# Polynomial-sketch attention and an ELU feed-forward on one core: the head of the program reordered

## The chip, the core and the metric

The kernel runs on one core of a Trainium2 chip. A core has five engines that run their own instruction streams and wait for each other by semaphores: PE (TensorE, matrix products; its weight loads are shown as PEld), DVE (VectorE), ACT (ScalarE), POOL (GpSimd) and SP (SyncE, which here only issues DMAs). ACT issues a few DMAs too. The metric is the device time of one execution in microseconds (us).

## The reference

q, k, v and the output are float32. The sketch matrices S1 and S2 and the two weights arrive as float64, and the kernel rounds them to float32 itself (see below).

```python
# q, k, v: (4, 4, 1088, 32)   S1, S2: (8, 32)   w_in: (128, 2048)   w_out: (2048, 128)
def phi(x):
    a = einsum('rd,bhsd->bhsr', S1, x)
    b = einsum('rd,bhsd->bhsr', S2, x)
    return einsum('bhsi,bhsj->bhsij', a, b).reshape(..., 64)
kv  = einsum('bhsf,bhsd->bhfd', phi(k), v)
z   = sum(phi(k), axis=2)
x   = einsum('bhsf,bhfd->bhsd', phi(q), kv) / (einsum('bhsf,bhf->bhs', phi(q), z) + 1e-6)
x   = x.transpose(0, 2, 1, 3).reshape(4352, 128)
h   = x @ w_in
g   = where(h > 0, h, exp(min(h, 0)) - 1)
out = g @ w_out
```

For each of four batches b, the keys and values of the whole sequence must be summed into kv and z before any query of that batch can be finished; the feed-forward part then takes the rows of x in groups.

## The kernel before

**Tiling.** The 4 x 1088 rows of x are 68 half tiles of 64 rows; eight of them make a group g of 512 rows (nine groups, the last has 256). The 2048 hidden columns are eight pairs cp of two blocks of 128. A step is one (g, cp): `mm1` makes two 128x512 blocks of h on PE, `elu` makes e on ACT (a relu of -h, then an exp) and gg on DVE, and `mm2` adds the pair's contribution into o on PE. The main loop runs `mm1` of step n, then the extra work hung on that step, `elu` of step n, and `mm2` of step n-2.

**The order is written out by hand.** Nothing is rescheduled: each engine runs its instructions in the order in which the source issues them, and the semaphores come from the tiles' dependences. So where a call stands in the source decides what it is queued behind on its engine.

**The head** is what stands before that loop (L603 to L647). It makes the first kv and z, the first group of x and the first two steps:

- The loads are issued first: S1 and S2, the keys of batch 0 in two parts (SP takes half tiles 0 to 8, ACT the others), eight half tiles of queries (`load_hd`, L143 and L144, SP one half and ACT the other, 128 KB each), v of batch 0 in two parts (`load_v(0)`), and then the weights pair by pair between the rest of the queries and the next batches. A DMA semaphore is one of eight in turn; a load waits until the load eight places before it in the list has landed.
- `keep_warm(n, cols)` multiplies a constant tile into a PSUM tile called idle that nobody reads (L223): n products of cols columns that only keep PE working.
- DVE rounds S (L102 to L128) and copies it to Sx. PE turns it (sps, L252, and SXps, L244), and DVE makes Sab of it (L254).
- `transp` on DVE (L237) turns the loaded keys and queries into kT and qT.
- `KF` (L276): products abp of kT and Sab; `KF_out` copies them to ab on ACT (L285); `KO` (L261) makes the outer products kp on DVE, in three parts; `KA` (L309) sums kp and v into kv on PE; `KC` (L321), `KZ1` (L330), `KS` (L345) and `KZ2` (L337) prepare kv and z for the queries.
- The first group of queries goes another way than the later ones: `q1_first` (abqp, L417, and abq, L421), `q2_first` (qp, L261), `q4_first` (transposes qtp, L434, and their copies qpT, L435), `q5_first` (x0ps, L456; dn and xn on DVE; x0tp, L471; xg, L472), `mm1_first` (L536).
- `x0_eps` (L441) opens the sums in x0ps: two products of one row (128x264 out, one partition in) put the 1e-6 of the reference into the two PSUM tiles to which L456 adds.

**Rounding of the weights.** The weights arrive as 64-bit words in raw; each is turned into float32 in five steps: `round_a` (DVE, L102), `round_b` (ACT, L107), `round_c` (DVE, L115 and L116), `round_d` (DVE, L120) and `round_e` (DVE, L128, or POOL for later pairs). RA(i), RB(i) and RC(i) are steps a, b and c to e of the i-th piece in the list `order` at L167. Pieces 0 and 1 are w_in of pairs 0 and 1, pieces 2 and 3 are w_out of pairs 0 and 1, piece 4 is w_in of pair 2.

**The second half of the head** (L625 to L647) interleaves the rounding of pieces 1, 2 and 3 with e and gg of steps (0,0) and (0,1), and with the second group of queries: `q2(1, 2)` (DVE, qp in two halves), `q4(1)` (transposes L486, copies L487), `q5(1, True)` (xps, L507) and `q5_out` (xg, ACT L518 and DVE L519), then one more `keep_warm(1)`. The main loop's first product is `mm1(1, 0)`; RC(3) hangs on its first step, RA(4) and RB(4) follow on that step, and RC(4) hangs on the next; piece 4 is first needed at `mm1(0, 2)`.

Of the kernel before, what the change touches and what calls it, by code (L numbers as in the profile page):

```python
# [27 lines left out]
def kernel(  # L28
# [19 lines left out]
    nc = tc.nc  # L48
# [18 lines left out]
    hd = {}  # L67
# [3 lines left out]
    kT = [const.tile([FD, NT, 64], F32, name=f"kT{b}") for b in range(B)]  # L71
    qT = [const.tile([FD, NT, 64], F32, name=f"qT{b}") for b in range(B)]

    def load_hd(eng, x, src, b, t0, t1, c=slice(0, 2)):
        if (x, b) not in hd:
            hd[x, b] = work.tile([P, 2, NT, D], F32, name="hd_" + x, tag="hd_" + x)
        eng.dma_start(hd[x, b][:, c, t0:t1, :],
                      src[b].rearrange("h (a c t) d -> (h a) c t d", a=32, c=2)[:, c, t0:t1, :])

    def load_v(b, engs=(nc.sync, nc.sync)):  # L80
        for u, eng in enumerate(engs):
            t0, t1 = u * KT, min(NT, u * KT + KT)
            r = slice(64 * u, 64 * u + 64)
            src = v[b].rearrange("h (y t) d -> y h t d", t=NT)[:, :, t0:t1, :]
            if b == 0:
                eng.dma_start(vt[b][r, :VN].rearrange("p (h t d) -> p h t d", h=H, t=KT)[:, :, :t1 - t0, :], src)
            else:
                for h in range(H):
                    eng.dma_start(vt[b][r, h * KT:h * KT + t1 - t0, :D], src[:, h])
# [50 lines left out]
            eng.dma_start(S16[rs, :], src)  # L140
    load_hd(nc.sync, "k", k, 0, 0, KT)
    load_hd(nc.scalar, "k", k, 0, KT, NT)
    load_hd(nc.sync, "q", q, 0, 0, 8, slice(0, 1))  # L143
    load_hd(nc.scalar, "q", q, 0, 0, 8, slice(1, 2))  # L144
    load_v(0)
    warm = const.tile([R, 1], F32, name="warm")
    nc.vector.memset(warm[:], 0.0)
# [21 lines left out]
    def round_w(f, i, *a):  # L169
        if wide:  # L170
            cp, w_in, w_out = order[i]
            c = slice(0 if w_in else 2 * P, 4 * P if w_out else 2 * P)
            f(raw_w[cp][:, c], W[:, cp, c], *a)

    def RA(i):
        round_w(round_a, i)

    def RB(i):
        round_w(round_b, i)

    def RC(i, pool=False):
        round_w(round_c, i)
        round_w(round_d, i)
        round_w(round_e, i, pool)
# [36 lines left out]
    def keep_warm(n, cols=256):  # L221
        for i in range(n):
            nc.tensor.matmul(idle[:, :cols], some[:, :P], some[:, :cols], skip_group_check=True)  # L223
# [12 lines left out]
    def transp(dst, x, b, t0, t1):  # L236
        nc.vector.transpose(dst[b][:, t0:t1, :].rearrange("p t (a c) -> p c t a", c=2), hd[x, b][:, :, t0:t1, :])  # L237
# [10 lines left out]
    Sab = const.tile([FD, H, 2 * R], F32, name="Sab")  # L248
    SW = const.tile([FD, B, H, 3, R], F32, name="SW")
    keep_warm(3)  # L250
    sps = psum.tile([P, 512], F32, name="sps", tag="aux")
    nc.tensor.matmul(sps[:, :2 * R], Sx[:].rearrange("p h d -> p (h d)"), ident[:2 * R, :2 * R])  # L252
    make_SX()
# [34 lines left out]
    def KO(b, gi):  # L288
        ab, rows = feats[b, gi]
        n = len(KG[gi])  # L290
        kp = work.tile([P, 4, H, R, R], F32, name="kp", tag="kp", bufs=3)
        outer(kp[:rows, :n].rearrange("p t h i j -> p (t h) i j"),
              ab[:rows, :n].rearrange("p t h x r -> p (t h) x r"))
        feats[b, gi] = kp, rows
# [62 lines left out]
    def half_tile(g, i, u):  # L357
        return divmod(8 * g + (2 * i + u if g < NQ - 1 else u * qn[g] + i), NT)
# [33 lines left out]
    def q2(g, parts=1):  # L392
        m = H * qn[g]
        x = abw[g][:, :m, :]
        pw = pws[g % 2]
        nc.vector.tensor_mul(pw[:, :m, :R], x[:, :, R:2 * R], x[:, :, 2 * R:])
        den = work.tile([P, 4 * H], F32, name="den", tag="den")
        nc.vector.tensor_reduce(den[:, :m], pw[:, :m], axis=AX, op=ADD)
        nc.vector.reciprocal(den[:, :m], den[:, :m])
        an = work.tile([P, 4 * H, R], F32, name="an", tag="an")  # L400
        nc.vector.tensor_mul(an[:, :m], x[:, :, R:2 * R], _ap(den[:, :m], [[1, m], [0, R]]))
        qp[g] = work.tile([P, 4 * H, R, R], F32, name="qp", tag="qp", bufs=2)
        for i in range(parts):
            h = slice(i * m // parts, (i + 1) * m // parts)
            a_ = an[:, h]
            b_ = x[:, h, :R]
            nc.vector.tensor_mul(qp[g][:, h], _ap(a_, list(a_.ap[1:]) + [[0, R]]),  # L407
                                 _ap(b_, [b_.ap[1], [0, R], b_.ap[2]]))
# [3 lines left out]
    def q1_first():  # L412
        p = psum.tile([P, 512], F32, name="abqp", tag="aux")
        for i in range(4):
            for u in range(2):
                b, t = half_tile(0, i, u)
                nc.tensor.matmul(p[64 * u:64 * u + 64, i * 64:i * 64 + 64], qT[b][:, t, :],  # L417
                                 Sab[:].rearrange("p h y -> p (h y)"),
                                 skip_group_check=True, tile_position=(0, 64 * u))
        x = work.tile([P, 4 * H, 2, R], F32, name="abq", tag="abq", bufs=1)  # L420
        nc.scalar.copy(x[:].rearrange("p m x r -> p (m x r)"), p[:, :4 * 64])  # L421
        abw[0] = x
# [14 lines left out]
    def x0_eps():  # L437
        xps = []
        for tt in range(2):
            p = psum.tile([P, 512], F32, name="x0ps", tag="h", bufs=4)  # L440
            nc.tensor.matmul(p[:, :8 * (D + 1)], some[:1, :P], eps[:].rearrange("p m d -> p (m d)"),  # L441
                             start=True, stop=False, skip_group_check=True)
            xps.append(p)
        return xps
# [45 lines left out]
    def q5(g, between=False):  # L490
        nh = qn[g] // 2
        xp = [psum.tile([P, 512], F32, name="xps", tag="aux") for _ in range(2)]

        parts = {0: [], 1: []}
        for w in range(2):
            for m in range(nh):
                b, b1 = (half_tile(g, 2 * m + w, u)[0] for u in range(2))
                if b != b1:
                    parts[w] += [(b, m, 1, slice(0, 64)), (b1, m, 1, slice(64, P))]
                elif parts[w] and parts[w][-1][0] == b and parts[w][-1][3] == slice(0, P):  # L500
                    parts[w][-1] = (b, parts[w][-1][1], parts[w][-1][2] + 1, slice(0, P))
                else:
                    parts[w] += [(b, m, 1, slice(0, P))]
        for h in range(H):
            for w in range(2):
                for b, m0, m, s in parts[w]:
                    nc.tensor.matmul(xp[w][D * h:D * h + D, :nh * P].rearrange("p (m s) -> p m s", s=P)[:, m0:m0 + m, s],  # L507
                                     kvS[64 * w:64 * w + 64, b, h, :], qpT[g][64 * w:64 * w + 64, h, m0:m0 + m, s],
                                     skip_group_check=True, tile_position=(64 * w, D * h))
        xg[g] = work.tile([P, 512], F32, name="xg", tag="xg", bufs=2)  # L510
        if not between:
            q5_out(g, xp)
        return xp

    def q5_out(g, xp):
        nh = qn[g] // 2
        to = xg[g][:, :2 * nh * P].rearrange("p (m w s) -> p w m s", w=2, s=P)
        nc.scalar.copy(to[:, 0], xp[0][:, :nh * P].rearrange("p (m s) -> p m s", s=P))  # L518
        nc.vector.tensor_copy(to[:, 1], xp[1][:, :nh * P].rearrange("p (m s) -> p m s", s=P))  # L519
# [11 lines left out]
    def mm1_first():  # L531
        hs[0, 0] = [psum.tile([P, 512], F32, name="h", tag="h", bufs=4) for c in range(2)]
        for tt in range(2):
            for c in range(2):
                s = slice(256 * tt, 256 * tt + 256)
                nc.tensor.matmul(hs[0, 0][c][:, s], W[:, 0, c * P:c * P + P], xg[0][:, s], skip_group_check=True)  # L536

    def elu_a(g, cp, c, parts=(0, 1)):

        n = qn[g] * P  # L540
        if c == 0 and 0 in parts:
            es[g, cp] = work.tile([P, 2, 512], F32, name="e", tag="e", bufs=2)
        e = es[g, cp][:, c, :n]
        if 0 in parts:
            nc.scalar.activation(e, hs[g, cp][c][:, :n], RELU, scale=-1.0)  # L545
        if 1 in parts:
            nc.scalar.activation(e, e, EXP, scale=-1.0)  # L547
# [52 lines left out]
            eng.dma_start(rows[b, :, t:t + n, :], o[64 * u:64 * u + 64])  # L600


    keep_warm(2, 192)  # L603
    transp(kT, "k", 0, 0, KT)
    transp(kT, "k", 0, KT, NT)
    KF(0)
# [1 line left out]
    transp(qT, "q", 0, 0, 8)  # L608
    KO(0, 0)
    q1_first()  # L610
    x0 = x0_eps()
    KO(0, 1)
    KO(0, 2)
    RA(0)
# [8 lines left out]
    q5_first(x0)  # L623
    mm1_first()
    RC(1)  # L625
    for c in range(2):
        elu_a(0, 0, c)
    mm1(0, 1)
    q2(1, 2)
    RA(2)  # L630
    RB(2)
    q4(1)
    for c in range(2):
        elu_d(0, 0, c)
    round_w(round_c, 2)
    x1 = q5(1, True)
    elu_a(0, 1, 0, (0,))
    q5_out(1, x1)
    keep_warm(1)
    elu_a(0, 1, 0, (1,))  # L640
    elu_a(0, 1, 1)
    round_w(round_d, 2)
    round_w(round_e, 2)
    for c in range(2):
        elu_d(0, 1, c)
    RA(3)
    RB(3)  # L647

# [106 lines left out]
```

## Time and profile before

| | us |
|---|---|
| median of 5 runs (290.19 to 291.64) | 291.29 |
| the profiled execution | 291.05 |
| its span, first to last instruction | 289.3 |
| PE busy in the span | 282.9 |
| ACT, DVE busy | 187.2, 166.4 |
| first key product abp (L276) starts | 6.88 |
| first product of the main loop (L529) starts | 24.05 |

Times in the profile count from the start of the span. A row of a timeline is a run of like instructions of one engine: start, time from the first start to the last end, engine, source line, operation, what it writes and reads, shape, count, and in brackets how long the engine had been idle and what released it. A float32 product is two records on PE. Records of PE overlap: what counts is the distance between starts, not a record's length, in which the way through the array is contained.

### The profile page before, as it was taken

To read this page: it belongs to the slowest core of one execution; us is meant where nothing else is said; L and a number is where in the kernel's file an instruction comes from. 1 tells how busy PE (TensorE), PEld (TensorE's weight loads), DVE (VectorE), ACT (ScalarE), POOL (GpSimd) and SP (SyncE) were. 2 spreads that over 40 slices of the span, in tenths; PEclk is the share of its full clock that TensorE was granted. 3 is DMA by queue.
4 is the path that set the end of the run, shared out by engine and by line. 5 is a ranking of instruction groups with operands and counts; after the bars stand their busy time and mean duration, and the time that the engine had idled before them with its cause. 6 is when DMAs were issued, how large, how long until landed. Compare 5 with 4: busy or idle time off the path is not lost.

```text
span 289.3 us, 3955 instructions
## 1 busy us (share of the span) xinstructions
PE 282.9 (98%) x1432; PEld 148.9 (51%) x1432; DVE 166.4 (58%) x298; ACT 187.2 (65%) x357; POOL 17.1 (6%) x49
## 2 busy tenths in 40 slices
PE   8999999999999999999999999999999999999994
PEld 5874354545544755445444554444445544444694
DVE  6887999794865393545355443464442654355442
ACT  2468878476575565656676658665766676568682
POOL 3100003433000101000000000000000000000000
PEclk9999999999999999999999999999999999999999
DMA  6997894200004000002001100020002000100020
GB/s 181 346 260 188 192 222 48 77 0 0 2 0 62 13 0 3 0 6 35 0 0 20 17 2 0 1 35 2 0 0 36 2 2 0 25 11 0 6 33 18
DMA packets 37282, 13.36 MB, mean 46 GB/s; under 512 B 31760, under 2 KB 35472, under 8 KB 37264
## 3 DMA queue, kind: packets, MB, share of 16 engines
q1 hardware_dynamic: 36752, 12.66, 19.3%
q10 hardware_dynamic: 512, 0.46, 0.5%
q8 instruction: 11, 0.18, 0.3%
q14 instruction: 7, 0.06, 0.1%
HBM read 10.88 MB, written 2.23 MB: 45 GB/s over the span
## 4 chain that ended last, share of the span: by engine, by line
PE 94%; DVE 2%; ACT 2%; issue 0%
PE h L529 38%; PE o L566 38%; PE kv L309 3%; PE ol L589 2%; PE xps L507 2%; PE qtp L486 2%; PE abp L276 2%; PE idle L223 2%; PE abwp L376 1%; PE abwp L380 1%; ACT e L547 1%; DVE gg L553 1%; PE x0ps L456 1%; ACT e L545 1%; PE h L536 0%; PE x0ps L441 0%
## 5 line engine op out<-in xcount | busy, mean ns | idle before, releaser
L553 DVE SCALAR_TENSOR_TENSOR gg<-e,h 128x512 f32<-128x512 f32 (+1 forms) x144 | 93.1, 656 | 105.5 <-ACT e L547 105.4
L529 PE MATMUL h<-xg,W 128*128 128x512 f32 (+1 forms) x284 | 126.9, 569 | 0.6 <-DVE W L128 0.6
L566 PE MATMUL o<-gg,W 128*128 128x512 f32 x256 | 121.9, 598 | 0.0
L545 ACT ACTIVATE e<-h 128x512 f32<-128x512 f32 (+1 forms) x144 | 81.4, 565 | 34.0 <-PE h L529 32.8
L547 ACT ACTIVATE e<-e 128x512 f32<-128x512 f32 (+1 forms) x144 | 87.3, 606 | 4.6
L529 PEld LDWEIGHTS h<-xg,W 128*128 128x128 f32 x284 | 53.3, 190 | 62.9 <-issue 55.0
L566 PEld LDWEIGHTS o<-gg,W 128*128 128x128 f32 x256 | 46.6, 190 | 50.3 <-issue 48.9
L487 ACT COPY qpT<-qtp 128x512 f32<-128x512 f32 (+1 forms) x16 | 8.1, 560 | 15.5 <-PE qtp L486 15.5
L387 ACT COPY abw<-abwp 128x384 f32<-128x384 f32 (+1 forms) x8 | 3.7, 459 | 18.4 <-PE abwp L376 8.7
L261 DVE TENSOR_TENSOR kp<-ab 128x1024 f32<-128x1024 f32 (+1 forms) x12 | 12.1, 1041 | 1.2 <-ACT ab L285 1.2
L309 PEld LDWEIGHTS kv<-v,kp 128*64 128x64 f32 (+1 forms) x288 | 9.1, 137 | 1.7 <-ACT e L545 0.8
L309 PE MATMUL kv<-v,kp 128*64 128x33 f32 (+3 forms) x288 | 9.8, 224 | 0.0
L107 ACT ACTIVATE W<-W,ebias 128x256 uint32<-128x256 uint32 (+1 forms) x11 | 6.6, 596 | 4.7 <-DVE W L102 4.5
L407 DVE TENSOR_TENSOR qp<-an,abw 128x1024 f32<-128x1024 f32 (+1 forms) x9 | 9.3, 1047 | 0.3
L486 PEld LDWEIGHTS qtp<-ident,qp 128*128 128x128 f32 x60 | 7.1, 141 | 4.2 <-issue 4.2
L518 ACT COPY xg<-xps 128x256 f32<-128x256 f32 (+1 forms) x8 | 2.9, 360 | 9.1 <-PE xps L507 9.1
L589 PEld LDWEIGHTS ol<-W,gg 128*128 128x128 f32 x64 | 8.1, 192 | 0.3
L589 PE MATMUL ol<-W,gg 128*128 128x128 f32 x64 | 8.1, 275 | 0.0
L486 PE MATMUL qtp<-ident,qp 128*128 128x128 f32 x60 | 7.9, 273 | 0.0
L507 PE MATMUL xps<-qpT,kvS 64*32 64x256 f32 (+2 forms) x176 | 6.7, 316 | 0.4 <-ACT qpT L487 0.4
L125 POOL TENSOR_TENSOR raw<-raw,tiny 128x512 f32<-128x512 f32 x4 | 4.2, 1044 | 42.7 <-DVE raw L120 38.8
L507 PEld LDWEIGHTS xps<-qpT,kvS 64*32 64x32 f32 x176 | 3.2, 105 | 6.3 <-ACT e L547 5.3
(89 smaller groups left out, 133.1 us busy)
## 6 DMA issues: line engine op xcount, KB each, us to landing
raw<-in_moe_w_in_dram SPq DMA_DIRECT2D x8, 256.0 KB, 5.8
raw<-in_moe_w_out_dram SPq DMA_DIRECT2D x8, 256.0 KB, 6.1
hd_k<-in_k_dram SPq DMA_DIRECT2D x3, 544.0 KB, 6.3
hd_q<-in_q_dram SPq DMA_DIRECT2D x3, 544.0 KB, 4.1
out_dram<-ob SPq DMA_DIRECT2D x40, 32.0 KB, 1.6
v<-in_v_dram SPq DMA_DIRECT2D x12, 72.0 KB, 5.9
v<-in_v_dram SPq DMA_DIRECT2D x12, 64.0 KB, 3.4
hd_k<-in_k_dram SPq DMA_DIRECT2D x1, 288.0 KB, 3.5
```

The lines of the kernel that those rows point to most:

```text
L261: nc.vector.tensor_mul(dst, _ap(a_, list(a_.ap[1:]) + [[0, R]]), _ap(b_, [b_.ap[1], [0, R], b_.ap[2]]))
L309: nc.tensor.matmul(kv[64 * hp:64 * hp + 64, g2, :n], kp[:rows, j, h].rearrange("p i j -> p (i j)"), _ap(vt[b][:rows, off:off + D], [[VN - ...
L407: nc.vector.tensor_mul(qp[g][:, h], _ap(a_, list(a_.ap[1:]) + [[0, R]]), _ap(b_, [b_.ap[1], [0, R], b_.ap[2]]))
L486: nc.tensor.transpose(p[:, o:o + P], qp[g][:, r:r + 2].rearrange("p t i j -> p (t i j)"), ident[:])
L487: nc.scalar.copy(qpT[g][:, 2 * hh:2 * hh + 2, :nh, :], p[:, :2 * nh * P].rearrange("p (h m s) -> p h m s", h=2, m=nh))
L507: nc.tensor.matmul(xp[w][D * h:D * h + D, :nh * P].rearrange("p (m s) -> p m s", s=P)[:, m0:m0 + m, s], kvS[64 * w:64 * w + 64, b, h, :], ...
L529: nc.tensor.matmul(hs[g, cp][c][:, :n], W[:, cp, c * P:c * P + P], xg[g][:, :n])
L545: nc.scalar.activation(e, hs[g, cp][c][:, :n], RELU, scale=-1.0)
L547: nc.scalar.activation(e, e, EXP, scale=-1.0)
L553: nc.vector.scalar_tensor_tensor(gs[g, cp][:, c, :n], es[g, cp][:, c, :n], -1.0, hs[g, cp][c][:, :n], op0=ADD, op1=MAX)
L566: nc.tensor.matmul(ops[g][:, :n], W[:, cp, (2 + c) * P:(3 + c) * P], gg[:, c, :n], start=(first and c == 0), stop=(last and c == 1))
L589: nc.tensor.matmul(ops[g][i][:], gg[:, c, i * P:i * P + P], W[:, cp, (2 + c) * P:(3 + c) * P], start=(first and c == 0), stop=(last and c ...
```

## The change

The program's head is reordered in four places; what is computed stays the same.

1. Loads: the first eight half tiles of queries come in one load on ACT's queue instead of two on SP's and ACT's. On SP v of batch 0 follows the keys directly.
2. PE: one filler product of 160 columns is added behind the first three, ahead of sps. The two filler products of 192 columns ahead of abp go, and the two products of `x0_eps` stand there. They stood behind abqp and ahead of kv.
3. Rounding of piece 2: RA(2) and RB(2) stand ahead of e of step (0,0) instead of behind the second group's q2.
4. Rounding of piece 3: RA(3) moves ahead of the second group's xps, RB(3) ahead of steps d and e of piece 2. The first relu of step (0,1), which stood ahead of xg, is issued behind it with the rest of e.

In order of instructions, DVE runs RA(2) ahead of L396 and RA(3) between L116 of piece 2 and L519; ACT runs RB(2) ahead of the first L545, and L518 ahead of all four instructions of e of step (0,1), with RB(3) behind these as before. SP issues one load fewer and PE one filler product fewer; the counts on the other engines stay.

```diff
-    def load_hd(eng, x, src, b, t0, t1, c=slice(0, 2)):
+    def load_hd(eng, x, src, b, t0, t1):
...
-        eng.dma_start(hd[x, b][:, c, t0:t1, :],
-                      src[b].rearrange("h (a c t) d -> (h a) c t d", a=32, c=2)[:, c, t0:t1, :])
+        eng.dma_start(hd[x, b][:, :, t0:t1, :],
+                      src[b].rearrange("h (a c t) d -> (h a) c t d", a=32, c=2)[:, :, t0:t1, :])
...
     load_hd(nc.scalar, "k", k, 0, KT, NT)
-    load_hd(nc.sync, "q", q, 0, 0, 8, slice(0, 1))
-    load_hd(nc.scalar, "q", q, 0, 0, 8, slice(1, 2))
+    load_hd(nc.scalar, "q", q, 0, 0, 8)
     load_v(0)
...
     keep_warm(3)
+    keep_warm(1, 160)
     sps = psum.tile([P, 512], F32, name="sps", tag="aux")
...
-    keep_warm(2, 192)
+    x0 = x0_eps()
     transp(kT, "k", 0, 0, KT)
...
     q1_first()
-    x0 = x0_eps()
     KO(0, 1)
...
     RC(1)
+    RA(2)
+    RB(2)
     for c in range(2):
         elu_a(0, 0, c)
     mm1(0, 1)
     q2(1, 2)
-    RA(2)
-    RB(2)
     q4(1)
     for c in range(2):
         elu_d(0, 0, c)
     round_w(round_c, 2)
+    RA(3)
     x1 = q5(1, True)
-    elu_a(0, 1, 0, (0,))
     q5_out(1, x1)
     keep_warm(1)
-    elu_a(0, 1, 0, (1,))
-    elu_a(0, 1, 1)
+    for c in range(2):
+        elu_a(0, 1, c)
+    RB(3)
     round_w(round_d, 2)
     round_w(round_e, 2)
     for c in range(2):
         elu_d(0, 1, c)
-    RA(3)
-    RB(3)
```

## The prediction

> **What bounds the kernel now.** First the page's engine rows and the chain that ended last.
>
> ```profile
> PE 282.9 (98%) x1432; PEld 148.9 (51%) x1432; DVE 166.4 (58%) x298; ACT 187.2 (65%) x357; POOL 17.1 (6%) x49
> ...
> PE 94%; DVE 2%; ACT 2%; issue 0%
> ```
>
> PE carries 94% of the chain, so only what lets PE start its steady work sooner can count. I therefore read PE's timeline of the first 36 us (start, length, engine, line, tiles, count of records; every product makes two).
>
> ```profile
> 1.19 2.93 PE L223 MATMUL idle<-some 128*128 128x256 f32 x6 [1.19 <-DVE warm L147]
> 4.18 0.58 PE L252 MATMUL sps<-ident,Sx 16*128 16x16 f32 x2
> 4.60 0.77 PE L244 MATMUL SXps<-Sx,idr 8*128 8x128 f32 x2
> 5.30 1.65 PE L223 MATMUL idle<-some 128*128 128x192 f32 x4
> 6.88 1.84 PE L276 MATMUL abp<-Sab,kT 128*64 128x64 f32 x33
> ...
> 9.17 1.15 PE L441 MATMUL x0ps<-eps,some 1*128 1x264 f32 x4
> 10.26 2.46 PE L309 MATMUL kv<-v,kp 128*64 128x64 f32 x72
> ...
> 24.05 1.95 PE L529 MATMUL h<-xg,W 128*128 128x512 f32 x4
> ...
> 31.72 1.98 PE L529 MATMUL h<-xg,W 128*128 128x512 f32 x4 [0.57 <-DVE W L128]
> ```
>
> After 24.05 the products follow each other without a wait over 0.1, except the one at 31.72. So the end is the start at 24.05, plus that stall of 0.57, plus fixed work; I sum the change as the shift of these two. Next, DVE's timeline.
>
> ```profile
> 4.79 0.23 DVE L254 TENSOR_TENSOR Sab<-sps,bmask 128x64 f32<-128x64 f32 x1 [0.76 <-PE sps L252]
> 4.93 1.36 DVE L237 STREAM_TRANSPOSE kT<-hd_k 128x576 f32<-128x576 f32 x2
> 6.53 0.71 DVE L237 STREAM_TRANSPOSE qT<-hd_q 128x512 f32<-128x512 f32 x1 [0.23 <-DMA hd_q<-in_q_dram]
> 8.45 2.69 DVE L261 TENSOR_TENSOR kp<-ab 128x1024 f32<-128x1024 f32 x3 [1.21 <-ACT ab L285]
> ...
> 11.27 1.21 DVE L261 TENSOR_TENSOR qp<-abq 128x1024 f32<-128x1024 f32 x1
> ...
> 26.12 0.28 DVE L102 TENSOR_SCALAR W<-raw 128x256 uint32<-128x256 uint32 x1
> 26.98 0.42 DVE L115 SCALAR_TENSOR_TENSOR W<-raw,W 128x256 uint32<-128x256 uint32 x1 [0.57 <-ACT W L107]
> ```
>
> kT is ready at 6.29 (4.93 + 1.36), yet abp starts at 6.88: the filler (L223, 192 columns) holds it. From 8.45 DVE runs without a gap to the end of qp at 12.48. Last, the clock, from the rows of two lines that issue products of one shape (min/median/max ns; first and last start).
>
> ```profile
> L276 PE MATMUL abp<-Sab,kT x34: 221/314/369, 6.9 to 8.6; 128*64 128x64 f32 x34
> ```
>
> ```profile
> L417 PE MATMUL abqp<-Sab,qT x16: 222/222/270, 8.5 to 9.0; 128*64 128x64 f32 x16
> ```
>
> One 64-column record takes 314 ns before about 8.3 us and 222 after. The starts say the same: records of 256 columns stand 0.43 apart at first (1.77, 2.20, 2.63 in finer slices of the timeline), and 0.32 apart with 192 columns (5.78, 6.10, 6.42): 1.67 ns a column. The x0ps records with 264 columns, at 9.5 to 9.9, stand 0.22 apart: 0.84 ns a column. So PE works at half its clock until 8.3 (the page's clock row prints full speed throughout; the durations say otherwise).
>
> **The change part by part**, against the profiled execution: span 289.3, time 291.05, so 1.75 lie around the span. The median of the five runs is 291.29, 0.24 above it.
>
> *Added filler, behind L250.* One product of 160 columns is two records of 160 x 1.67 ns = 0.27, so 0.53. It stands ahead of sps. The last 256-column record starts at 3.48 and frees PE at 3.91; sps starts at 4.18, when Sx is ready, so 0.27 of the filler lies in this wait and 0.26 delays sps, SXps and Sab. The second kT transpose then ends at 6.55.
>
> *x0ps in the filler's place.* Four records of 264 columns replace four of 192. At half clock they take 4 x 0.44 = 1.76 instead of 4 x 0.32 = 1.28. They start at 5.30 + 0.26 = 5.56 and end at 7.32; with the 0.14 that PE loses today between filler and abp (6.42 + 0.32 to 6.88) abp starts at 7.46, **0.58 late**. Its first 16 records, which the first ab copy waits for, start 0.0535 apart; the last two or three fall past 8.3, where pairs stand 0.058 apart instead of 0.107. So the first ab comes 0.52 late and kp starts at 8.97 instead of 8.45. Bounds if the clock differs: nothing to 0.62 late, or earlier by the second rival.
>
> *What that takes out behind abqp.* x0ps no longer stands at 9.17 to 10.26. kv needs kp's first part: 8.97 + 1.23 = 10.2, about where kv starts today. kv then no longer binds: qtp waits for qp, which ends at 12.48 + 0.52 = 13.0. Today qtp starts at 12.65, 0.17 behind qp, because kv is still running; released straight by qp it needs some 0.08. So qtp starts at 13.08, **+0.42**, and with it ACT's copy of qpT, the second x0ps products (L456) and the first h. DVE waits 0.56 for these products ahead of L464, so its rounding does not hold them. If the clock were as now but abp not late, this step alone would give 0.1.
>
> *The loads.* ACT issues 256 KB of queries in one go (L77) where SP and ACT issued 128 KB each; SP passes on to v one issue (0.59) sooner, and every later load of SP waits for the load eight back in a list one shorter. Bytes and order stay, apart from half the queries, and the queues are busy from 3.5 to 20 us, so I cost the later loads at nothing. Queries: ACT's 128 KB today flow from 5.0 to 5.6 beside SP's and have landed at 6.5; another 128 KB at that rate end 0.6 later, so they land at 7.1 and are transposed by 7.8, under the wait for ab until 8.97. That cover is 1.2 us. v landed at 7.88 and 8.87 and comes earlier; kv asks for it at 10.2, so this also buys nothing.
>
> *RA(2) and RB(2) ahead of e.* RA(2) on DVE (0.25 from start to start) delays q2 of group 1; qp's second half is ready at 21.09 instead of 20.84 and PE's second half of qtp slips 0.08. RB(2) on ACT (0.49) goes into ACT's wait of 0.79 for the first h, starting when RA(2) is done (18.49) and ending 0.14 behind 18.80; e goes late by 0.14. It leaves the place ahead of qpT at 21.12. The copy then waits for PE (21.35) rather than for RB(2) (21.51): **-0.10** for qpT, xps and the start at 24.05. Bounds 0 and -0.16.
>
> *e behind xg, RA(3) and RB(3).* The first half of e of pair (0,1) moves out of ACT's idle time before xg; the second gg then waits for 26.09 instead of 25.48, 0.61 later. But RA(3) (0.28) sits in DVE's wait for xps, and RB(3) runs on ACT at 26.0 to 26.5 while gg runs. Today DVE does gg (to 26.20), RA(3), then waits 0.57 for RB(3), and L115 starts at 26.98. Now it starts behind gg: 26.12 + 0.60 = 26.72. That chain, RC(3), gg twice, RC(4), ends the stall at 31.72, so **-0.26**. The stall shrinks from 0.57 to about 0.3. Bounds: 0 (e's delay eats it all) and -0.57 (stall gone).
>
> Sum: +0.42 - 0.10 - 0.26 = +0.06, time 291.05 + 0.06 = **291.1**.
>
> [...]
>
> **Rivals.**
>
> *Full clock before abp.* The filler closes PE's hole between 3.91 and 5.30, and PE gets its clock by 5.6 already. For it: PE then works nearly unbroken from 1.2 to 7.3, and one of the five runs is 1.1 below the median with the same code, about what this would be worth. Against: sps and SXps stay a stretch of 1.1 with 0.3 of columns in it. Price: x0ps takes 1.08 (as today at full clock) and ends at 6.64; kT is ready at 6.55; abp starts at about 6.75. Sixteen records take 0.46, the last 0.22 until done, the copy 0.42: kp starts at 7.85, 0.60 earlier, and qtp 0.70 with the 0.1 above. Sum -0.70 - 0.10 - 0.26 = -1.06: **290.0**. Queries that land after 7.1 would take some of it.
>
> *Clock full much later (slower).* x0ps reads one row (1x264); no row shows whether such products count as work toward the clock, for today they run after 8.3. If not, PE is without work from 5.6 to 7.3, and after abqp it has none until kp. Then kv runs at half clock: 2.39 x 107/58 = 4.4 instead of 2.39, from 10.2 to 14.6, 1.95 behind today's 12.65. Time: 291.05 + 1.95 - 0.36 = **292.6**. It decides from a clock that is half until about 11.1: from there on kv ends later than qp's 13.0; until about 13 the loss stays within what can be told. For it: the hole in front of kp. Against: v and kp wait alike, and four products in their place today did not hold the clock down.
>
> *Nothing gained at 31.72.* e behind xg costs what RB(3) saves; only the +0.42 and -0.10 remain: **291.4**. For it: 0.61 against 0.57 on paper. Against: DVE's gg overlaps RB(3).
>
> *Loads do it.* If v or the queries bound the head, the new order would move kv by up to 1. Against: kv starts at 10.26, 1.4 after v. I count it at nothing.
>
> **How the numbers follow.** Likeliest, 0.46: the clock as now, 291.1 (290.6 to 291.7 by the bounds above). First rival, 0.31: 290.0. Second, 0.13: 292.6. Third, 0.10: 291.4. Some 0.3%, 0.87 around 291.29, is what a measurement here can tell from no change: 290.42 to 292.16. Faster: 0.31 and 0.04 from the likeliest's lower edge, 0.35. Slower: 0.13 and 0.02 from upper edges, 0.15. Same: 0.50. The range leaves out the slower rival and tails of the first: 289.6 to 292.0. The predicted time is 291.1.
>
> **What would show it.** Right, if abp starts near 7.5 with 314 ns records first, kv waits for kp and not for x0ps, qtp starts near 13.1, RB(2) lies ahead of 18.9, L115 of the third rounding starts 0.3 after gg's last start or sooner, and the stall at the first product of W's third pair is about 0.3. The first rival shows as abp records of 222 ns from its start. The second shows as kv records above 0.3. I am wrong altogether if the head ends later than 24.5 with a full clock, or if the time moves by over 0.9 while the start at 24.05 does not.

## The result and the profile after

The changed kernel takes 292.03 us (median of 43 runs, 291.13 to 293.34); the kernel before, beside it, 291.31 (80 runs, 289.97 to 294.92). The ratio is 1.0033 with a 95% interval of 1.0024 to 1.0043: slower by 0.96 us (0.72 between the two medians), where 291.1 and "no change" were forecast, and just above the range of the prediction (289.6 to 292.0).

The spread tells more than the median. Of the 80 runs of before, 20 lie between 289.97 and 290.35, the next one at 290.97; none of the 43 after is below 291.13. At the other end 13 of the 43 are above 292.3, and 4 of the 80.

The profiled executions are closer together: 291.45 after (span 289.7), 291.05 before (289.3). First the page's PE row and the head of the chain that ended last.

```profile
PE 283.4 (98%) x1430; PEld 149.6 (52%) x1430; DVE 166.3 (57%) x298; ACT 187.3 (65%) x357; POOL 17.1 (6%) x49
...
PE 91%; DVE 3%; DMA 2%; ACT 1%; ACTq 0%; issue 0%
```

PE has 91% of the chain instead of 94%, and DMA, which had no share that the page prints before, has 2%. The chain's row by lines names the load: hd_q, the first queries. PE's timeline (start, length, engine, line, tiles, count of records) shows where the head stands:

```profile
5.59 1.96 PE L441 MATMUL x0ps<-eps,some 1*128 1x264 f32 x4
7.49 2.18 PE L276 MATMUL abp<-Sab,kT 128*64 128x64 f32 x34
9.49 1.04 PE L417 MATMUL abqp<-Sab,qT 128*64 128x64 f32 x16
10.50 2.67 PE L309 MATMUL kv<-v,kp 128*64 128x64 f32 x72
13.39 1.06 PE L434 MATMUL qtp<-ident,qp 128*128 128x128 f32 x8 [0.23 <-DVE qp L261]
...
24.65 1.95 PE L529 MATMUL h<-xg,W 128*128 128x512 f32 x4
...
32.06 1.98 PE L529 MATMUL h<-xg,W 128*128 128x512 f32 x4 [0.30 <-DVE W L128]
```

abp starts at 7.49 and not 6.88, qtp at 13.39 and not 12.65, the main loop at 24.65 and not 24.05. The stall at the third pair is 0.30 and not 0.57. DVE's timeline shows who holds kp, and through it kv and qtp:

```profile
8.63 0.71 DVE L236 STREAM_TRANSPOSE qT<-hd_q 128x512 f32<-128x512 f32 x1 [1.90 <-DMA hd_q<-in_q_dram]
9.26 2.65 DVE L261 TENSOR_TENSOR kp<-ab 128x1024 f32<-128x1024 f32 x3
...
26.75 0.69 DVE L553 SCALAR_TENSOR_TENSOR gg<-e,h 128x512 f32<-128x512 f32 x1 [0.46 <-ACT e L547]
27.35 0.42 DVE L115 SCALAR_TENSOR_TENSOR W<-raw,W 128x256 uint32<-128x256 uint32 x1
```

The queries land at 8.60, 2.1 later than before. DVE waits 1.90 for them and turns them into qT; kp stands behind that in DVE's order. The first ab, which kp also needs, was done sooner, by ACT's timeline:

```profile
8.66 0.37 ACT L285 COPY ab<-abp 128x256 f32<-128x256 f32 x1 [2.56 <-PE abp L276]
```

That is 9.03, so 0.23 of kp's delay is the queries' own. Last, the clock, by the two lines that issue one shape (min/median/max ns, first and last start):

```profile
L276 PE MATMUL abp<-Sab,kT x34: 314/314/368, 7.5 to 9.4; 128*64 128x64 f32 x34
```

```profile
L417 PE MATMUL abqp<-Sab,qT x16: 234/314/369, 9.5 to 10.3; 128*64 128x64 f32 x16
```

All of abp and nearly all of abqp are at half clock (314 ns; 222 is full). The rise is at 10.3, against 8.3 in the trace of before.

### The profile page after: what moved, and what is told of

It is laid out like the page before. It is cut to its first block, busy times and chain, and to the rows that moved or that the text cites. A ratio compares the mean times of both kernels' runs of the same rounds, so it can differ in the third digit from the quotient of the medians.

```text
span 289.7 us, 3949 instructions
## 1 busy us (share of the span) xinstructions
PE 283.4 (98%) x1430; PEld 149.6 (52%) x1430; DVE 166.3 (57%) x298; ACT 187.3 (65%) x357; POOL 17.1 (6%) x49
## 4 chain that ended last, share of the span: by engine, by line
PE 91%; DVE 3%; DMA 2%; ACT 1%; ACTq 0%; issue 0%
PE h L529 39%; PE o L566 38%; PE ol L589 2%; PE kv L309 2%; DMA hd_q<-in_q_dram 2%; PE xps L507 2%; PE qtp L486 2%; PE abwp L376 1%; PE abp L276 1%; PE abwp L380 1%; DVE kp L261 1%; PE x0ps L456 1%; DVE gg L553 1%; PE h L536 1%; ACT e L547 0%; DVE qp L261 0%
## 5 line engine op out<-in xcount | busy, mean ns | idle before, releaser
L545 ACT ACTIVATE e<-h 128x512 f32<-128x512 f32 (+1 forms) x144 | 81.4, 565 | 33.2 <-PE h L529 32.8
L518 ACT COPY xg<-xps 128x256 f32<-128x256 f32 (+1 forms) x8 | 2.9, 359 | 9.6 <-PE xps L507 9.6
L236 DVE STREAM_TRANSPOSE qT<-hd_q 128x1088 f32<-128x1088 f32 (+2 forms) x5 | 5.4, 1085 | 1.9 <-DMA hd_q<-in_q_dram 1.9
```

## The experiments

Fourteen kernels were run. Before's median beside them was 291.40 to 291.66. First all of them in one table: what the traces show, in us from the start of the span ("clock" is when PE's products first reach full speed, which e2 and e13 lose again later, "q" when the transpose of the first queries starts, "main" the first product of the loop), and the timed comparison with before.

| run | clock | abp | q | kp | kv | qtp | main | median | ratio [95%] |
|---|---|---|---|---|---|---|---|---|---|
| before | 8.3 | 6.88 | 6.53 | 8.45 | 10.26 | 12.65 | 24.05 | 291.31 | |
| after | 10.3 | 7.49 | 8.63 | 9.26 | 10.50 | 13.39 | 24.65 | 292.03 | 1.0033 [1.0024, 1.0043] |
| e1_loads | 10.6 | 6.94 | 8.46 | 9.10 | 11.54 | 13.93 | 25.32 | 293.77 | 1.0072 [1.0040, 1.0105] |
| e2_filler | 4.3 | 5.98 | 6.49 | 7.55 | 8.90 | 12.27 | 23.66 | 291.55 | 0.9992 [0.9965, 1.0019] |
| e3_round | 8.7 | 6.86 | 6.73 | 8.44 | 10.40 | 12.80 | 24.08 | 291.31 | 0.9987 [0.9960, 1.0015] |
| e4_noloads | 10.7 | 7.49 | 6.64 | 9.06 | 10.34 | 13.23 | 24.48 | 290.89 | 0.9983 [0.9954, 1.0011] |
| e5_q_ahead | 13.3 | 7.49 | 7.60 | 9.06 | 10.34 | 14.07 | 25.36 | 291.86 | 1.0026 [1.0006, 1.0046] |
| e6_q_behind_v | 10.7 | 7.48 | 9.10 | 9.73 | 10.97 | 13.86 | 25.12 | 292.18 | 1.0046 [1.0025, 1.0067] |
| e7_v_behind_w | 13.1 | 7.48 | 9.02 | 9.66 | 11.27 | 14.47 | 25.75 | 292.82 | 1.0067 [1.0032, 1.0102] |
| e8_no160 | 12.6 | 7.01 | 7.06 | 8.59 | 9.87 | 13.48 | 24.76 | 290.86 | 1.0005 [0.9985, 1.0026] |
| e9_full_rows | 4.9 | 6.44 | 8.87 | 9.50 | 10.74 | 13.63 | 24.89 | 291.60 | 1.0016 [0.9999, 1.0033] |
| e10_full_rows_noloads | 4.1 | 6.10 | 6.71 | 7.48 | 9.15 | 11.65 | 22.96 | 291.51 | 0.9996 [0.9969, 1.0022] |
| e11_one_row_filler | 4.5 | 5.76 | 6.45 | 7.39 | 9.11 | 11.56 | 22.98 | 293.42 | 1.0076 [1.0040, 1.0111] |
| e12_sx_behind | 6.5 | 7.26 | 6.65 | 8.40 | 9.68 | 12.58 | 23.84 | 290.25 | 0.9955 [0.9935, 0.9976] |
| e13_v_far | 10.4 | 7.48 | 8.04 | 9.05 | 12.68 | 15.97 | 27.72 | 294.39 | 1.0085 [1.0051, 1.0120] |
| e14_sx_behind_no160 | 4.4 | 6.11 | 6.59 | 7.42 | 9.18 | 11.59 | 22.91 | 291.21 | 0.9978 [0.9956, 0.9999] |

A caution for reading it: a trace is one execution, and the mean clock on record differs from run to run of one kernel (0.988 to 1.0 in those of the change). Between kernels the columns can be compared only where the clock is alike. From the main loop's first product to the end all traces have 265.0 with the moved rounding and 265.2 without, so "main" decides.

### The parts alone, and the change without its loads

e1_loads: before, with the loads of the change alone.

```diff
-    load_hd(nc.sync, "q", q, 0, 0, 8, slice(0, 1))
-    load_hd(nc.scalar, "q", q, 0, 0, 8, slice(1, 2))
+    load_hd(nc.scalar, "q", q, 0, 0, 8)
```

> The kernel before with the change's loads alone (first queries in one load on ACT's queue, v behind the keys on SP's); PE's order and the rounding as before. Theory Q (queries travel beside v and land at 8.6 instead of 6.5, so kp cannot start before 9.3 whatever PE's clock does): qT transposed from about 8.6, kp from 9.3 instead of 8.45, and the time 0.6 to 0.9 above before, 291.9 to 292.2; no run near the fastest of before (290.0). Theory P (the filler that now takes 264 instead of 192 columns holds abp, the loads are covered): queries may land late but the time stays within 0.2 of before, with fast runs near 290.0.

Measured: 293.77 (12 runs, 292.05 to 297.16), ratio 1.0072 [1.0040, 1.0105]. The loads alone are the loss, and more than it: 291.9 to 292.2 was expected. PE's timeline of this kernel says why more:

```profile
9.32 1.12 PE L416 MATMUL abqp<-Sab,qT 128*64 128x64 f32 x16 [0.20 <-DVE qT L236]
10.38 1.23 PE L440 MATMUL x0ps<-eps,some 1*128 1x264 f32 x4
11.54 2.46 PE L308 MATMUL kv<-v,kp 128*64 128x64 f32 x72
```

abqp waits for the late qT, x0ps stands behind abqp, and kv behind x0ps: 11.54 instead of 10.26. In the changed kernel x0ps is out of that line, and kv starts as soon as kp is there (10.50). The execution traced is one of the quicker ones (292.38); what the eight of 12 runs above 293 lose beyond it is in no trace.

e2_filler: before, with the order of PE of the change alone.

```diff
     keep_warm(3)
+    keep_warm(1, 160)
...
-    keep_warm(2, 192)
+    x0 = x0_eps()
...
     q1_first()
-    x0 = x0_eps()
```

> The kernel before with PE's order alone (160 columns of filler ahead of sps, x0_eps in place of the two fillers of 192 columns); loads and rounding as before. Theory Q: abp starts 0.6 late in runs at half clock, kp starts about 9.0, the time 0.1 to 0.5 above before, 291.4 to 291.8, and runs whose clock is full early are still near 290. Theory P: this part holds the whole loss, 0.9 to 1.3 above before, 292.2 to 292.6.

Measured: 291.55 (12 runs, 289.97 to 292.53), 0.9992 [0.9965, 1.0019]: no change that can be told. This trace shows the clock go full early and fall again; columns are the window, its length, then busy time and count of PE, PEld, DVE, ACT and POOL, the granted clock, DMA's share and GB/s:

```profile
4.30:7.60 3.30, 3.17 (x46) 2.34 (x44) 2.26 (x5) 0.67 (x3) 0.88 (x6) 1.00 1.05 288
7.70:11.00 3.30, 3.05 (x56) 2.89 (x58) 3.30 (x5) 1.31 (x4) 0.00 (x0) 0.50 1.06 335
11.10:14.00 2.90, 2.90 (x50) 2.59 (x47) 2.59 (x7) 1.46 (x5) 0.89 (x4) 1.00 1.08 364
```

PE is busy by its records for 3.17 of 3.30 in the first stretch, and yet the second runs at half clock. What filled the first is sps, SXps, the one-row x0ps and abp.

e3_round: before, with the rounding of pieces 2 and 3 and the place of e of the change alone.

```diff
     RC(1)
+    RA(2)
+    RB(2)
...
-    RA(2)
-    RB(2)
...
+    RA(3)
...
-    elu_a(0, 1, 0, (0,))
     q5_out(1, x1)
     keep_warm(1)
-    elu_a(0, 1, 0, (1,))
-    elu_a(0, 1, 1)
+    for c in range(2):
+        elu_a(0, 1, c)
+    RB(3)
...
-    RA(3)
-    RB(3)
```

> The kernel before with the moved rounding and e alone. Both theories: a gain, by my sum 0.36 (0.10 at qpT, 0.26 at the stall of 0.57 at the third pair's first product), 290.9; stall about 0.3. If the later e eats it: 291.3 and the stall unchanged.

Measured: 291.31 (12 runs), 0.9987 [0.9960, 1.0015]; timing can't tell it from nothing. The trace can: from qtp to the main loop 11.28 instead of 11.40 (24.08 - 12.80), and the stall 0.307 instead of 0.568.

e4_noloads: the changed kernel with the two loads of queries as before.

```diff
-    load_hd(nc.scalar, "q", q, 0, 0, 8)
+    load_hd(nc.sync, "q", q, 0, 0, 8, slice(0, 1))
+    load_hd(nc.scalar, "q", q, 0, 0, 8, slice(1, 2))
```

> The changed kernel with the loads of before (queries in two halves ahead of v). Theory Q: the loss goes away, 291.0 to 291.2, 0.8 to 1.0 below the changed kernel, queries land at 6.5, kp starts at about 9.0 in a run with half clock until past 8. Theory P: it stays where the changed kernel is, 291.8 to 292.2.

Measured: 290.89 (12 runs, 290.04 to 292.13), 0.9983 [0.9954, 1.0011]. With the loads undone the loss is gone, and six of twelve runs lie at 290.04 to 290.59; in the 43 of the changed kernel none is below 291.13. In the trace qT starts at 6.64 and kp, as predicted, waits for ab alone (9.06); the main loop starts at 24.48, 0.17 sooner than after, at nearly the same clock (10.7 and 10.3). So one such execution shows a sixth of a microsecond, and the comparison of all runs 1.4 (292.03 / 291.31 against 290.89 / 291.54). The other runs need another explanation, for which the next groups were made.

### What makes the queries late

Three kernels move the loads in the changed kernel: the queries in one load on SP ahead of v (e5), on SP behind v (e6), and v behind the first weights of SP's list (e7).

```diff
# e5_q_ahead
-    load_hd(nc.scalar, "q", q, 0, 0, 8)
+    load_hd(nc.sync, "q", q, 0, 0, 8)
     load_v(0)
# e6_q_behind_v
-    load_hd(nc.scalar, "q", q, 0, 0, 8)
     load_v(0)
+    load_hd(nc.sync, "q", q, 0, 0, 8)
# e7_v_behind_w
     load_hd(nc.scalar, "q", q, 0, 0, 8)
-    load_v(0)
...
     load_w(0, 0)
+    load_v(0)
```

> The changed kernel with its one load of queries issued by SP behind its keys and ahead of v, instead of by ACT. Theory V (it is the company of v that slows the queries: in both traces packets take 75 to 100 ns while v flows, 46 to 51 otherwise): queries land at 6.4 to 7.0, packets of 46, kp starts when ab is ready (9.0 in a run at half clock), the time 290.7 to 291.3. Theory L (one load of 256 KB is slow as such, or because one queue carries it): they land past 7.5, the time 291.5 to 292.0.

> The changed kernel with its one load of queries put on SP behind both halves of v: a larger dose of the suspected delay, PE's order untouched. Theory V/Q (the landing of the queries opens the kp chain): they land at about 8.7 to 9.5 and kp starts 0.7 behind that landing; every 0.1 that they land later than 8.6 costs 0.1 over the changed kernel, so 292.0 to 293.0. If the queries do not bind: no change to the changed kernel, 292.0.

> The changed kernel with v behind the first weights on SP; the queries still one load on ACT, beside those weights (packets of 2 KB to 128 partitions). Theory V (v's shape, 64 partitions a load, slows what travels beside it): queries land at 6.3 to 6.9, v at 9.5 to 10, in time for kv; the time 290.7 to 291.4. If any neighbour slows them: land past 7.5, 291.6 to 292.1.

Measured: e6, 292.18 (11 runs), 1.0046 [1.0025, 1.0067], is a dose of the same delay: the queries land 0.48 later than after (9.08), kp starts 0.47 later (9.73) and the main loop 0.47 later (25.12), at a clock like after's. So, with the queries later than ab, their 0.48 arrives at the main loop almost whole.

e7, 292.82 (7 runs), 1.0067 [1.0032, 1.0102], speaks against v as the only cause: v is further back and the queries still land at 9.0, where 6.3 to 6.9 was expected if v was it. And now kv waits for v, which lands at 11.13.

e5, 291.86 (11 runs), 1.0026 [1.0006, 1.0046], brings the queries in at 7.57, in time for ab, and is not faster than before. Its kp starts at 9.06 like e4's, and then kv is slow: the same 72 records, first in e5, then in e4:

```profile
L309 PE MATMUL kv<-v,kp x72: 218/314/368, 10.3 to 13.9; 128*64 128x64 f32 x64, 64*64 64x64 f32 x8
```

```profile
L310 PE MATMUL kv<-v,kp x72: 218/222/369, 10.3 to 12.8; 128*64 128x64 f32 x64, 64*64 64x64 f32 x8
```

In e5 the clock stayed half until 13.3, in e4 until 10.7: 1.1 us of kv. So e5's time, which is what was expected if a single load is late as such (291.5 to 292.0), is no verdict on its loads.

e13_v_far takes v out of the way altogether: behind the first weights, the other queries and the second weights.

```diff
-    load_v(0)
...
     load_w(1, 0)
+    load_v(0)
     load_w(1, 1)
```

> The changed kernel with v three loads further back on SP (behind the first weights, the other queries and the second weights); queries still one load on ACT. Theory V (only v's company slows the queries): packets of queries at 46 ns and landing at 6.4 to 7.2; kp starts when ab is ready, 9.0 at half clock; v lands past 11, so kv is late and the time no better (292 to 293.5). If one load on ACT is late whatever it travels beside: landing past 8.

Measured: the queries land at 8.02, 0.58 sooner than after, but still 1.5 later than before. The time, 294.39 (6 runs), 1.0085 [1.0051, 1.0120], is v's, as PE's timeline shows:

```profile
12.68 3.37 PE L309 MATMUL kv<-v,kp 128*64 128x64 f32 x72 [2.16 <-DMA v<-in_v_dram]
```

The DMA view of 5 to 6 us shows what there is of it (packets, rate, then each queue's packets, MB and time as a share of 16 engines; q1 is SP's, q10 ACT's). After:

```profile
DMA packets 204, 0.21 MB, mean 211 GB/s; under 512 B 14, under 2 KB 204, under 8 KB 204
...
q1 hardware_dynamic: 138, 0.14, 77.4%
q10 hardware_dynamic: 66, 0.07, 34.6%
```

Before:

```profile
DMA packets 327, 0.33 MB, mean 326 GB/s; under 512 B 28, under 2 KB 327, under 8 KB 327
...
q1 hardware_dynamic: 195, 0.21, 73.3%
q10 hardware_dynamic: 132, 0.12, 34.1%
```

By these shares a packet takes 88 ns of an engine after (1.12 x 16 us / 204), with v on SP's queue, and 53 before (1.07 x 16 / 327), where SP's queue has queries until 5.3 and v from 5.2, and ACT's has queries until 5.7. ACT's queue moves 0.07 MB, in e13 0.15. In e13 another thing holds the landing: of the 560 packets of ACT's queue all but nine have started by 6.83, and the nine follow one at a time, 0.09 apart, until 7.63. What the runs settle: the new place and form of the loads makes the queries 2 us late. What v's company has in that is not settled: 0.6 by one pair of traces (e13 and after), nothing by another (e7, 9.0). What of the rest is the sharing with SP's other loads, and what the single load in place of two, stays open too.

### What holds the clock down

In e5 and e8 PE was filled by products for a whole stretch (e5: busy by the profile without a break from 6.51 to 9.92), and the clock stayed half until 13.3 and 12.6. The suspects are the products of one row, x0ps: the change puts them in the place of the fillers, which have 128 rows. e8_no160 is e4 without the 160 columns. e9_full_rows is the changed kernel, e10_full_rows_noloads e4, with x0ps of 128 rows; all but the first row are zero, so the sums stay the same.

```diff
# e8_no160 (from e4)
-    keep_warm(1, 160)
# e9_full_rows (from after), e10_full_rows_noloads (from e4)
-    eps = const.tile([1, 8, D + 1], F32, name="eps")
+    eps = const.tile([P, 8, D + 1], F32, name="eps")
     nc.gpsimd.memset(eps[:], 0.0)
-    nc.gpsimd.memset(eps[:, :, D:], 1e-6)
+    nc.gpsimd.memset(eps[:1, :, D:], 1e-6)
...
-            nc.tensor.matmul(p[:, :8 * (D + 1)], some[:1, :P], eps[:].rearrange("p m d -> p (m d)"),
+            nc.tensor.matmul(p[:, :8 * (D + 1)], some[:, :P], eps[:].rearrange("p m d -> p (m d)"),
```

e11_one_row_filler is before with nothing changed but the rows of its two fillers ahead of abp, 1 instead of 128.

```diff
-    def keep_warm(n, cols=256):
+    def keep_warm(n, cols=256, rows=P):
...
-            nc.tensor.matmul(idle[:, :cols], some[:, :P], some[:, :cols], skip_group_check=True)
+            nc.tensor.matmul(idle[:, :cols], some[:rows, :P], some[:rows, :cols], skip_group_check=True)
...
-    keep_warm(2, 192)
+    keep_warm(2, 192, 1)
```

> The version with the loads of before and the rest of the change (290.9 measured) without the added filler of 160 columns. By my sum the filler delays sps by 0.26 and abp with it: 0.26 faster at half clock, 290.6; abp at 7.2, kp at 8.8. If the filler earns its place through the clock (fewer runs with full clock by 4.5 without it): 291.0 to 291.4 and no early full clock.

> The changed kernel with the two products of x0_eps over 128 rows (the 1e-6 in row 0, zeros below) instead of one row: the same columns, length and result. [...] Theory N (rows make no difference): 291.9 to 292.1 with the same upper tail to 293.3.

> The same 128 rows, with the loads of before (the version at 290.9). [...] Theory N: 290.9.

> The kernel before with one row instead of 128 in the two fillers of 192 columns; nothing else. [...] Theory N: 291.3.

Measured. e11: 293.42 (8 runs: 289.98, 291.36, 291.42, and five at 293.27 to 294.6), 1.0076 [1.0040, 1.0111]. Two products that nobody reads, of the same columns, cost 2.0 us by their rows alone, more than was expected if the rows count (291.7 to 292.5). The one execution traced is the early one, 289.98, with the clock full from 4.5, so that the clock is what the others lose is inferred: two of them have a mean clock of 0.987 and 0.988, which fits one that fell again as in e2, the rest 0.997 to 1.0. e8 by its median (290.86, 1.0005 [0.9985, 1.0026]) doesn't tell the 160 columns from none, 290.89 in e4; its trace has the clock half until 12.6.

e9: 291.60 (12 runs), 1.0016 [0.9999, 1.0033]; eleven of twelve lie between 290.99 and 291.78, so the tail above 292.3 that the changed kernel has is all but gone, though its early runs do not come back. DVE's timeline of e9, whose clock is full by 4.9 and whose ab is done at 7.85, shows what stands there instead:

```profile
8.87 0.71 DVE L236 STREAM_TRANSPOSE qT<-hd_q 128x512 f32<-128x512 f32 x1 [2.16 <-DMA hd_q<-in_q_dram]
9.50 2.64 DVE L261 TENSOR_TENSOR kp<-ab 128x1024 f32<-128x1024 f32 x3
```

e10 is the same PE order with the loads of before, and DVE's timeline has:

```profile
6.71 0.71 DVE L237 STREAM_TRANSPOSE qT<-hd_q 128x512 f32<-128x512 f32 x1 [0.40 <-DMA hd_q<-in_q_dram]
7.48 2.69 DVE L262 TENSOR_TENSOR kp<-ab 128x1024 f32<-128x1024 f32 x3
```

kp 2.02 sooner, the main loop 1.93 sooner (22.96 and 24.89), both with an early clock. In e10 the clock is full 0.8 sooner (4.1 and 4.9) and the first ab done 0.4 sooner (7.45 and 7.85), so the queries' part is some 1.6: in e9 kp starts 1.65 behind its ab, in e10 0.03. That is the loads' price in a run with an early clock, against 0.17 in one with a late clock (after and e4). Five of e10's twelve runs lie at 289.71 to 290.07, none of e9's twelve is below 290.99. But e10's median is 291.51, 0.9996 [0.9969, 1.0022], a miss of what was expected if the rows count (290.2 to 290.7) and if not (290.9), and no better than e4 with its one-row products (0.9983 [0.9954, 1.0011]): six runs lie at 291.49 to 291.56. That the clock comes late in these is inferred; none of them was traced.

### A head that beats both

e12_sx_behind is e10 with SXps, which PE makes from Sx for later use, moved behind x0ps. sps and SXps, products of 16 and 8 rows, stood between the fillers and x0ps (4.37 to 5.01 in e10's trace, 4.58 to 5.59 after); now the ones of 128 rows follow sps directly. e14_sx_behind_no160 is e12 without the 160 columns.

```diff
# e12_sx_behind (from e10)
     nc.tensor.matmul(sps[:, :2 * R], Sx[:].rearrange("p h d -> p (h d)"), ident[:2 * R, :2 * R])
-    make_SX()
...
     x0 = x0_eps()
+    make_SX()
# e14_sx_behind_no160 (from e12)
-    keep_warm(1, 160)
```

> The version with the loads of before and 128 rows in x0_eps, with make_SX (8 rows) moved behind x0_eps, so that PE goes from sps straight into x0_eps. [...]

> The same as the first without the added filler of 160 columns. If those columns earn their place through the clock: more runs at 291 and above, median 290.5 to 291.3. If not: sps 0.26 earlier at half clock, 289.7 to 290.3.

Measured: e12 takes 290.25 (12 runs, eleven at 289.77 to 290.62), where 289.8 to 290.5 was expected, 0.9955 [0.9935, 0.9976]: 1.3 us faster than before and, by the two ratios, 2.3 faster than the change (0.0078 x 291.3). Of the 25 runs of before beside it one is below 291.0. Its trace, with the clock full from 6.5 (PE's timeline):

```profile
5.11 1.81 PE L441 MATMUL x0ps<-eps,some 128*128 128x264 f32 x4
6.85 0.48 PE L244 MATMUL SXps<-Sx,idr 8*128 8x128 f32 x2
7.26 1.26 PE L276 MATMUL abp<-Sab,kT 128*64 128x64 f32 x34
9.68 2.67 PE L309 MATMUL kv<-v,kp 128*64 128x64 f32 x72 [0.57 <-DVE kp L261]
...
23.84 1.96 PE L529 MATMUL h<-xg,W 128*128 128x512 f32 x4
```

abp runs at full clock throughout (1.26 for 34 records, 2.18 after). e14 takes 291.21, 0.9978 [0.9956, 0.9999], with two runs at 289.64 and 289.68 and ten at 291.15 to 291.53: the 160 columns earn their place, not by time of their own (the two early runs are the fastest of all) but by the share of runs in the early group. In e8 beside e4 the medians had not shown this; the early group had, for none of e8's eleven runs is below 290.50 and three of e4's twelve are at 290.04.

## Why the prediction was wrong

**The step that failed: "so I cost the later loads at nothing", and under it "they land at 7.1 and are transposed by 7.8, under the wait for ab until 8.97. That cover is 1.2 us."** They land at 8.60. The 0.6 that I added for another 128 KB took ACT's rate from a stretch in which SP's queue carried the other half of the queries; I moved v ahead on SP's queue and did not ask what either does to ACT's queue (why they are that late stays open in part, see e7 and e13). Nor did v come earlier as a whole: its second half landed at 9.56 instead of 8.87. The cover is then missed by 0.23 in the traced execution. It is missed by far more where the clock comes early and ab is done at 7.4 to 7.9: there the late queries cost some 1.6 us (e9 against e10). I had seen both halves of this, the gap of 1.1 between runs and the sentence that late queries would take some of the first rival's gain, and did not put them together: a load that is hidden in the usual run is bare in the fast one.

**The clock: the second rival was real, though not in the traced execution.** "Against: ... four products in their place today did not hold the clock down" compared products of 128 rows with products of one. That PE's clock follows its work, on which this rival and the first were built, was my estimate; the trace of before, with its one rise at 8.3, does not show it. In e2 and e13 the rises and falls stand some 3.4 apart (4.3, 7.7 and 11.1 in e2; 10.4, 13.85 and 17.3 in e13), so I count over stretches of that length, laid back to back from each trace's rise. They are a yardstick: no trace shows what the clock goes by. In a stretch, count the time that columns take (at half clock 0.427 for a record of 256, 0.107 for a pair of records of 64, gaps left out). In e5 the stretch from 6.51 to 9.92 is filled to 95%, 70% without the one-row products, and the clock stayed half; in e8 the one from 5.77 to 9.18 to 95% and 62%. Over all sixteen traces the stretches ahead of a rise hold 75 to 98% of 128-row columns (78 before, 80 after, 82 in e9, 81 in e10, 76 in e12), and those ahead of another stretch at half clock 15 to 75%. By all columns the two overlap (76 and more, up to 95). So in these traces 128-row columns tell the two apart, by my estimate from these shares near three quarters, and e11 shows the effect of the rows on the time by itself (+2.0). That the data of x0ps are almost all zeros is not the reason: in e12 they are too, over 128 rows, and make up 1.2 of the 2.6 us of columns in the stretch ahead of its rise. The rival's own sum was good: kv begun at 10.2 and at half clock until 13.3 ends at 13.3 + 2.39 - 3.1 x 58/107 = 14.0 by its rates, and e5's qtp starts at 14.07.

The profile's records do not tell these stretches apart: in e5 PE is busy by them without a break from 6.51 to 9.92, and the products stay at half clock until 13.3. The groups of before's runs are some 1.3 us apart, 0.4%, and that is more than the whole effect looked for.

**The sum, term by term, in the traced execution.** sps is 0.40 late (0.26 predicted), x0ps 0.30 (0.26), abp at 7.49 (7.46). kp at 9.26 (8.97): 0.06 because ab came at 9.03, 0.23 by the queries. qtp +0.74 (+0.42): 0.29 of the difference is kp. kv waits for kp and qtp for qp, as predicted. RA(2) and RB(2): -0.14 after and -0.12 in e3 (-0.10 predicted). The stall: -0.27 after (-0.26). Main loop +0.60 and stall -0.27 make +0.33; with some 0.08 of small differences behind it the span is +0.41. So the traced execution is off by the one term, and the rest of the 0.96 is runs that the trace does not show: the early ones that before has and after has not (e9 and e10 show why), and 13 of 43 above 292.3. The mean clock on record for each run says something of these. Traces with one rise have 0.997 or more, e2's and e13's, in which the clock falls again for some 3.4 us, 0.992 and 0.994. Eight of the 13 have 0.988 to 0.994, which fits a clock that fell again. The other five have 0.999 or 1.0, as a late rise has in e5 (0.999). With 128 rows in x0ps all but one such run are gone (e9), so the rows seem to be behind both kinds; no trace shows one of these runs.

**The first rival** (full clock before abp, 290.0) is what e2, e10, e11 and e14 show in their traces, with kp at 7.4 to 7.6 instead of the 7.85 that I had worked out. It is no property of the new order: by their times, before has it too in a quarter of its runs (20 of 80). **The third rival** fell: the rounding pays what was predicted. **"Loads do it"**, counted at nothing with the argument that kv starts 1.4 after v has landed, was the cause in the traced execution: the queries bound, as it said, but they came later and not sooner.

## What to carry to other kernels

Cost a moved load against the fastest run that the kernel has, not against the one in the profile: cover that is there only while something else is late is none (the late queries cost 0.17 in after against e4, some 1.6 in e9 against e10). A filler that is to keep the clock up, and anything put in a filler's place, should use all 128 rows (with one row in two fillers e11 was 2.0 us slower; what lies between was not tried by itself); count the columns of full-row products, of which the 3.4 us ahead of a rise held 75% or more in these traces. When two groups of runs lie 1 us apart, a change of the head is judged by which group its runs fall into, so look at all the times and not at the median or one trace.

## What the runs showed of the hardware

- Products of one row: in e5 the stretch from 6.51 to 9.92 is filled to 95% by all columns, 70% by those of 128 rows, with PE busy without a break by the profile, and the clock stayed half until 13.3; e11 was slower by 2.0 us by the rows of two products alone.
- The full clock was lost again with work in every stretch: in e2 it is full from 4.3 to 7.7, half to 11.1, full after that (granted clock 1.00, 0.50, 1.00), with PE busy for 3.17 and 3.05 of 3.30 in the first two; in e13 it falls at 13.85 after kv's wait of 2.16 for v, until 17.3. The 3.4 us before these falls hold 38% and 34% of 128-row columns; with its one-row products e2's hold 71%. In e9 those from 8.3 to 11.7 hold 42%, and the clock stayed full, where up to 75% in other traces came ahead of more half clock.
- From 5 to 6 us after, with v on SP's queue and queries on ACT's, a packet takes 88 ns of its engine, and both queues together move 211 GB/s; before, with queries on SP's queue until 5.3, v there from 5.2, and queries on ACT's until 5.7, it is 53 ns and 326 GB/s. In before the rate is nearly as low when SP's queue moves alone, v and from 7.2 the first weights: 251 and 240 GB/s from 6 to 8 us, against 379 from 4 to 5 with keys and queries.
